# Second layers loaded later, one feature product on GpSimd, and the first rows stored later

## The chip, the cores and the metric

The kernel runs on one core of a Trainium2 chip. The metric is the device time of one execution in microseconds, as the median over several runs. A profile of one execution is used to see what each engine did. In its views the engines are PE (TensorE), PEld (TensorE's weight loads), DVE (VectorE), ACT (ScalarE), POOL (GpSimd) and SP (SyncE); a q behind a name means the queue of that engine, from which it issues DMAs.

## The reference

```python
# attention: batch 4, heads 4, sequence 1088, head size 32, r = 8
def phi(x):                       # 64 features per row: all products of two sketches
    a = einsum('rd,bhsd->bhsr', S1, x);  b = einsum('rd,bhsd->bhsr', S2, x)
    return einsum('bhsi,bhsj->bhsij', a, b).reshape(..., 64)
q_p, k_p = phi(q), phi(k)
kv = einsum('bhsf,bhsd->bhfd', k_p, v);  z = sum(k_p, axis=2)
x = (einsum('bhsf,bhfd->bhsd', q_p, kv) / (einsum('bhsf,bhf->bhs', q_p, z)[..., None] + 1e-6))
x = x.transpose(0, 2, 1, 3).reshape(4352, 128)        # one row per token
# router and experts: 8 experts, 128 -> 1024 -> 128
logits = (x / (|x| + 1e-6)) @ (emb / (|emb| + 1e-6)).T / tau
expert = argmax(logits, 1);  gate = max(softmax(logits))
out[token] = gate[token] * (relu(x[token] @ w1[expert]) @ w2[expert])
```

The inputs are float32, except that S1 and S2 are float64 and are rounded on the chip. Only the expert with the highest score works on a token, so the kernel must sort the tokens by expert while it runs.

## The kernel before, in words

**Attention.** The four batches are taken as two pairs, m = 0 and m = 1. In a pair, tiles of tokens go through in groups of four (GROUPS; the last group has four and one rest tile). For the keys of a group (`keys`) TensorE transposes the rows, multiplies them with the sketch matrix into PSUM (`sketch`), ACT copies one of the two factors to SBUF (`second`, L377), VectorE multiplies the two factors into features of 128x1024 (`features`, L383), and TensorE adds keys times values into an accumulator (L432). For the queries (`queries`) the features are made in the same way (steps `tr`, `ab`, `b`, `prod`), then transposed on TensorE (`tr_qp`, L508), copied to SBUF by ACT (`qpT`, L514) and multiplied with the finished key-value matrix `kz` (`nd`, L522). `x` (L532 to L539) divides by the denominator into the row tile `xg`. The query features of pair 0 are kept in `held`, which is the memory that the second layers of experts 4 to 7 take later.

**Rows and tables.** Each row of `xg` holds 128 values, 8 shifted logits and a scale: `squares` sums squares on ACT (L544) and takes the root on GpSimd (L546); `store` inverts it, for the first eight tiles of a pair on GpSimd (L657, L658) and for the others on VectorE (L654, L655). `write` sends the rows to `rows` in DRAM, by SP (L662), and the rest tile by GpSimd (L666). The router (`best`, `pick`, `place`, `take`, `split`, `mark`) finds the expert of each token on VectorE as a one-hot (`pick`, L613) and its place among the tokens of that expert with a series of small matmuls on TensorE (`place`, L623 to L627, and L753). For pair 0 a table is then worked out (`plan_early`, `table`): `find` and `digit` on VectorE (L718, L722) make `hit` and `col`, `sums` on TensorE (L728) adds them up, and `tokens` on VectorE (L743 to L745) turns the sums into the indices `src_i`, by which full blocks of 128 tokens of one expert can be gathered.

**Experts.** `fetch` gathers a block's rows from `rows` by an indirect DMA on GpSimd (L861). `turn` transposes them (L867), `weights` copies the first layer into the order needed (L874), `up` runs the first layer in 16 passes (L917), `down` the second (L943), and the result goes out by an indirect DMA on GpSimd (L952). There are 36 blocks. The first ten hold tokens of pair 0 alone and start while pair 1 is still in its attention; the others use a second table. Four fetches are put ahead of the first block.

**Loads.** SP issues the loads: keys, queries, values, then all first layers (L180) and the second layers of experts 0 to 3 (L176). The second layers of experts 4 to 7 are eight loads of 256 KB into `held`.

**What sets the order.** Steps are put on a list as functions with a tick and a rank (`put_at(tick)(after, rank, step)`); `emit` runs the list sorted by tick and rank. For the engines that `manual_schedule` names, the instructions stand in the order in which they are emitted; for an engine that it doesn't name, a scheduler places them. In the kernel before, SP is not named. Each engine works off its instructions in order, and an instruction waits until what it reads is ready and what it overwrites has been used.

Of the kernel before, what the change touches and what calls it, by code (L numbers as in the profile page):

```python
# [11 lines left out]
F32 = mybir.dt.float32  # L12
BF16 = mybir.dt.bfloat16
# [6 lines left out]
P = 128  # L20
B, H, S, D = 4, 4, 1088, 32
R = 8
DM = H * D
N = B * S
E, F = 8, 1024
# [38 lines left out]
def kernel(  # L64
# [13 lines left out]
    nc = tc.nc  # L78
# [3 lines left out]
    consts = ctx.enter_context(tc.tile_pool(name="consts", bufs=1))  # L82
    rows_p = ctx.enter_context(tc.tile_pool(name="rows", bufs=4))
    work = ctx.enter_context(tc.tile_pool(name="work", bufs=2))
# [85 lines left out]
    held = w2_sb[:, E // 2:].rearrange("p e f d -> p e (f d)")  # L170

    def load_w2(e):

        for u in range(2):
            f = slice(u * NF // 2, (u + 1) * NF // 2)
            nc.sync.dma_start(w2_sb[:, e, f], w2[e].rearrange("(p f) d -> p f d", p=P)[:, f])  # L176
# [22 lines left out]
    top, rem, w, fits = word("s_top"), word("s_rem"), word("s_w"), word("s_fits")  # L199
# [144 lines left out]
    ND_AT = (range(n_g, 2 * n_g), range(2 * n_g, 3 * n_g))  # L344
# [30 lines left out]
    def second(ab, n, tag):  # L375
        b = tile_of(n, [P, n * H, R], tag)
        nc.scalar.copy(b, ab[:, :, 1])  # L377
        return b

    def features(ab, b, n, tag, t=None):  # L380
        if t is None:
            t = tile_of(n, [P, n, H, R * R], tag)
        nc.vector.tensor_mul(t.rearrange("p j h (i k) -> p (j h) i k", i=R),  # L383
                             ab[:, :, 0].unsqueeze(3).broadcast_to([P, n * H, R, R]),
                             b.unsqueeze(2).broadcast_to([P, n * H, R, R]))
        return t
# [91 lines left out]
    def queries(m, c0, c1, put, put_nd):  # L478
        n = c1 - c0
        w = n * P  # L480
        s = {}
# [12 lines left out]
        def ab():  # L494
            s["ab"] = sketch(ab_bank(put.tick, n, 0), s["qT"], n)

        def b():
            s["b"] = second(s["ab"], n, "qb")

        def prod():  # L500
            t = held[:, c0 // 4].rearrange("p (j h f) -> p j h f", j=4, h=H) if m == 0 and n > 1 else None
            s["qp"] = features(s["ab"], s["b"], n, "qp", t)

        def tr_qp():
            ps = ps_big() if n > 1 else ps_small().rearrange("p (b n) -> p b n", b=2)
# [43 lines left out]
        if m == 0:  # L549
            put(-1, 53, tr)  # L550
            put(0, 50, ab)
            put(0, 50.5, b)
            put(0, 54, prod)
            for i, f in enumerate((tr_qp, qpT)):
                put_nd(*((0, 47.7 + 0.02 * i) if c0 == 0 else (-1, 57)), f)
            put_nd(0, 70, nd)
            put_nd(0, 71.5 if n == 1 else 71, x)
            put_nd(*((1, 55.3 if n == 1 else 53.6) if last else (1, 53.5)), squares)
        else:

            at_rank = ({tr: (7, 53), ab: (7, 70.6), b: (7, 70.7), prod: (7, 71.2), tr_qp: (8, 55.5), qpT: (8, 58),
                        nd: (8, 84), x: (8, 90), squares: (9, 55)},
                       {tr: (8, 53.5), ab: (8, 55.8), b: (8, 58.7), prod: (8, 62.5), tr_qp: (9, 20), qpT: (9, 20),
                        nd: (9, 30), x: (9, 71), squares: (10, 53.5)},
                       {tr: (8, 55.3), ab: (8, 84.6), b: (8, 84.7), prod: (9, 20.2), tr_qp: (9, 30.2), qpT: (9, 30.6),
                        nd: (10, 70), x: (10, 71), squares: (11, 53.5)},
                       {tr: (8, 84.5), ab: (9, 21), b: (9, 30.7), prod: (10, 33), tr_qp: (11, 20), qpT: (11, 20),
                        nd: (11, 70), x: (11, 71), squares: (11, 77)})[min(step, 3)]
            for f, (t, rank) in at_rank.items():
                put_at(t)(0, rank, f)  # L570
        if c1 == s1:

            by = 1 if m == 0 else 2
            bank = (lambda: spare[m, 4 + 4 * by]) if c1 < NC else (lambda: table_bank[m][:, 0])
            best, pick, place, take, split, mark, store, write = router(m, s0, s1, g, bank)

            if m == 0 and c1 < NC:
                at_rank = {best: (0, 80), pick: (0, 81), place: (1, 70.5), take: (1, 71.2), split: (2, 54),
                           mark: (2, 54), store: (2, 54), write: (2, 55)}
            elif m == 0:  # L580
                at_rank = {best: (0, 80), pick: (0, 81), place: (1, 56), take: (1, 56.9), split: (1, 57),
                           store: (1, 57.2), write: (1, 58), mark: (1, 59)}
            elif c1 < NC:
                at_rank = {best: (1, 72), pick: (1, 72), store: (1, 86), write: (1, 90), place: (2, 70.5),
                           take: (2, 71.2), split: (4, 76.5), mark: (5, 76)}
            else:
                at_rank = {best: (1, 31), pick: (1, 31), place: (1, 75.1), take: (1, 76), split: (1, 76),
                           store: (2, 78), write: (2, 90), mark: (6, 32)}
            if c1 == NC:
                put_nd(at_rank[place][0], at_rank[place][1] - 0.1, lambda: table_bank.append(ps_big()))  # L590
            for f, (t, rank) in at_rank.items():
                put_nd(t, rank, f)
# [107 lines left out]
    def table(which, m1, key):  # L700

        n, w = SIZES[which] + which * SHARED, m1 * NCP
        s = {}

        def lie(t):
            return t if which == 0 else t.rearrange("p n w -> p w n")

        def find():  # L710
            if which == 0:
                s["hit"] = consts.tile([P, n, w], BF16, name="hit0")
                s["col"] = consts.tile([P, 2, n, w], BF16, name="col0")
            else:

                s["hit"] = work.tile([P, w, n], BF16, tag="xg", bufs=3, name="hit1").rearrange("p w n -> p n w")
                s["col"] = work.tile([P, w, 2, n], BF16, tag="xg", bufs=3, name="col1").rearrange("p w d n -> p d n w")
            nc.vector.tensor_tensor(out=lie(s["hit"]), in0=lie(key().unsqueeze(2).broadcast_to([P, n, w])),  # L718
                                    in1=lie(bview(place_k, [[0, n], [1, w]])), op=ALU.is_equal)

        def digit(d):
            nc.vector.tensor_mul(lie(s["col"][:, d]), lie(s["hit"]), lie(bview(digits[:, d], [[0, n], [1, w]])))  # L722

        def sums():
            s["ps"] = ps_small()[:, :2 * n]
            tiles = [m * NCP + c for m in range(m1) for c in range(NC)]
            for t in tiles:
                nc.tensor.matmul(s["ps"], row[:, :, t], s["col"].rearrange("p d n w -> p (d n) w")[:, :, t], start=t == tiles[0], stop=t == tiles[-1])  # L728

        def first_rows():  # L730
            s["b"] = consts.tile([HALF, 2, SHARED], BF16, name="halves")
            nc.vector.tensor_copy(s["b"], s["ps"].rearrange("p (d n) -> p d n", d=2)[:HALF, :, LATE:])

        def halves():

            ps = s["ps"].rearrange("p (d n) -> p d n", d=2)
            nc.tensor.matmul(ps[:, :, PAIRS:PAIRS + SHARED], down_half, s["b"], start=False, stop=True, skip_group_check=True)

        def tokens(k0, k1):
            ps = s["ps"].rearrange("p (d n) -> p d n", d=2)  # L740
            rest = column(f"rest{which}_{k0}", w=k1 - k0)
            to = dst_i[which][:, k0:k1]
            nc.vector.tensor_scalar(rest, ps[:, 1, k0:k1], -1.0, float(NOWHERE), op0=ALU.mult, op1=ALU.add)  # L743
            nc.vector.tensor_sub(to, rest, ps[:, 0, k0:k1])
            nc.vector.tensor_scalar_min(src_i[which][:, k0:k1], to, N - 1)  # L745
        return find, lambda: digit(0), lambda: digit(1), sums, tokens, first_rows, halves

    def tokens_by_expert(rounded, out):
# [213 lines left out]
    def put_at(tick):  # L962
        def put(after, rank, f):
            at.setdefault(tick + after, []).append((rank, len(at.get(tick + after, ())), f))
        put.tick = tick
        return put
# [14 lines left out]

    for i in range(n_g):

        put_at(ND_AT[0][-1])(1, 59.6, lambda i=i: load_w2(E // 2 + i))

    count, rest, others = plan_early()
    find, high, low, sums, tokens, *_ = table(0, 1, lambda: early["key"])
# [56 lines left out]

    def emit():
        with tc.manual_schedule(engines={mybir.EngineType.PE, mybir.EngineType.DVE, mybir.EngineType.Activation,
                                         mybir.EngineType.Pool}):
            for i in sorted(at):
                for _, _, f in sorted(at[i], key=lambda x: x[:2]):
                    f()  # L1050
        at.clear()
# [48 lines left out]
```

## Time and profile before

| what | value |
|---|---|
| median of three runs | 212.55 us (211.67 to 212.64) |
| the profiled execution's own time | 212.05 us |
| its span | 210.2 us (1.85 us lie around it) |
| granted TensorE clock | 0.998 of full speed |
| busy: PE, DVE, POOL, ACT | 196.2 (93%), 127.7 (61%), 107.6 (51%), 105.9 (50%) us |
| moved by DMA | 22.68 MB |
| L383, query features of 128x1024 on DVE | 1.21 us each |
| L658 on POOL, 128x8 | 1.67 us |
| loads of w2 and w1 | 32 of 256 KB, median 5.7 us to landing |
| writes of `rows` by SP | 4 of 548 KB, median 5.3 us to landing |
| gathers `xs` from `rows` | 36, median 2.6 us to landing |

All times in views of the trace are microseconds from the start of the span; a line of a timeline gives start, duration, engine, source line, operation, what is written and read, and in brackets how long the engine had been idle before and what ended that. The releaser that is named is the one that came last by the profile; what an instruction really waits for can be another one.

### The profile page before, as it was taken

The page shows a single profiled execution, that of the slowest core. Times are in us where ns is not written, and L with a number is a line of the kernel's source. Part 1 is how long each engine was busy: PE and PEld are TensorE (multiplying, and loading weights), DVE is VectorE, ACT ScalarE, POOL GpSimd, SP SyncE. Part 2 cuts the span into 40 slices and gives each one's busy share as a digit, 9 for nine tenths or more (in the row PEclk, how much of TensorE's full clock was granted, in tenths as well). Part 3 has the DMA queues.
Part 4 walks back from the last instruction along what each step waited for, and adds up shares of the span by engine and source line. Part 5 has one row for each costly group of instructions (what it writes and reads, how often), then busy time and mean ns, then how long its engine had stood idle before and what let it go on. Part 6 is the DMA issues. An engine that isn't in the chain of part 4 may idle for free.

```text
span 210.2 us, 6754 instructions
## 1 busy us (share of the span) xinstructions
PE 196.2 (93%) x2566; PEld 186.5 (89%) x2566; DVE 127.7 (61%) x368; ACT 105.9 (50%) x288; POOL 107.6 (51%) x116
## 2 busy tenths in 40 slices
PE   8969999988879999999999999999999999999991
PEld 7758889966768989998999999999999999999991
DVE  5985476898977786889545453544545356575300
ACT  2544477675559745354243535445353544676430
POOL 4101002163178795741578767676766767752322
PEclk9999999999999999999999999999999999999999
DMA  4979899999611301300111211101111120110000
GB/s 120 327 201 316 220 266 372 346 341 378 235 43 27 125 27 57 134 29 25 25 44 38 56 39 41 40 26 41 34 42 38 38 41 28 41 42 10 7 28 25
DMA packets 18369, 22.68 MB, mean 108 GB/s; under 512 B 5353, under 2 KB 12532, under 8 KB 18336
## 3 DMA queue, kind: packets, MB, share of 16 engines
q1 hardware_dynamic: 15904, 17.33, 25.4%
q0 software_dynamic: 2432, 4.90, 8.9%
q8 instruction: 22, 0.36, 0.8%
q14 instruction: 11, 0.09, 0.1%
HBM read 17.61 MB, written 4.74 MB: 106 GB/s over the span
## 4 chain that ended last, share of the span: by engine, by line
PE 58%; DVE 15%; issue 10%; DMA 4%; SPq 4%; ACT 3%; POOL 3%; POOLq 1%; DVEq 0%; ACTq 0%
PE ps_big L917 22%; PE ps_acc L943 10%; PE ps_ab L943 10%; DMA k_rest<-in_k_dram 3%; PE ps_big L522 2%; PE ps_big L508 2%; SPq L125 2%; PE ps_acc L432 2%; POOL out_dram L952 2%; PE ps_big L922 2%; PE ps_t L867 2%; PE ps_t L728 2%; DVE xg L534 2%; DVE wb L874 2%; SPq L135 1%
## 5 line engine op out<-in xcount | busy, mean ns | idle before, releaser
L952 POOL DMA_INDIRECT out_dram<-y,dst_i x36 | 49.4, 1372 | 37.5 <-ACT y L949 33.4
L917 PE MATMUL ps_big<-xTb,wb 128*128 128x128 f32 x512 | 63.1, 276 | 0.9 <-ACT xTb L870 0.4
L917 PEld LDWEIGHTS ps_big<-xTb,wb 128*128 128x128 f32 x512 | 59.7, 192 | 2.0 <-issue 1.0
L925 ACT ACTIVATE hT<-ps_big 128x1024 f32<-128x1024 f32 x36 | 36.8, 1023 | 48.1 <-PE ps_big L917 46.2
L861 POOL DMA_INDIRECT xs<-rows,src_i x36 | 37.6, 1043 | 19.5 <-issue 12.9
L874 DVE COPY wb<-w_sb 128x1024 f32 x35 | 38.6, 1103 | 11.3 <-issue 9.9
L943 PE MATMUL ps_acc<-w_sb,hT 128*128 x256 | 31.3, 276 | 0.0
L943 PE MATMUL ps_ab<-w_sb,hT 128*128 x256 | 31.2, 275 | 0.0
L943 PEld LDWEIGHTS ps_ab<-w_sb,hT 128*128 128x128 f32 x256 | 29.9, 192 | 0.0
L943 PEld LDWEIGHTS ps_acc<-w_sb,hT 128*128 128x128 f32 x256 | 29.8, 192 | 0.0
L934 DVE TENSOR_SCALAR gate<-gate 128x1 f32<-128x1 f32 x36 | 5.5, 152 | 30.2 <-ACT probs L931 30.2
L546 POOL TENSOR_TENSOR xg<-ssq,half_c 128x4 f32<-128x4 f32 (+1 forms) x10 | 9.8, 984 | 23.8 <-ACT sq L544 23.7
L870 DVE COPY xTb<-ps_t 128x128 f32<-128x128 f32 x30 | 8.7, 290 | 14.5 <-PE ps_t L867 14.4
L949 ACT ACTIVATE y<-ps_ab,gate 128x128 f32<-128x128 f32 x18 | 6.6, 367 | 12.6 <-PE ps_ab L943 11.0
L949 ACT ACTIVATE y<-ps_acc,gate 128x128 f32<-128x128 f32 x18 | 6.6, 367 | 10.4 <-PE ps_acc L943 8.8
L522 PE MATMUL ps_big<-kz,qpT 128*64 128x82 f32 x256 | 10.8, 236 | 0.9 <-issue 0.5
L522 PEld LDWEIGHTS ps_big<-kz,qpT 128*64 128x64 f32 x256 | 9.6, 136 | 2.0 <-issue 1.5
L544 ACT ACTIVATE sq<-xg 128x128 f32<-128x128 f32 x34 | 10.6, 311 | 1.2 <-DVE xg L534 0.4
L867 PE MATMUL ps_t<-ident,xs 128*128 128x128 f32 x36 | 10.2, 283 | 1.0 <-DMA xs<-rows,src_i 1.0
L931 ACT ACTIVATE probs<-xs 128x8 f32<-128x8 f32 x36 | 10.6, 294 | 0.0
L432 PE MATMUL ps_acc<-v,kp 128*64 128x64 f32 x256 | 9.2, 225 | 0.4 <-DVE kp L383 0.4
L432 PEld LDWEIGHTS ps_acc<-v,kp 128*64 128x64 f32 x256 | 8.1, 138 | 1.5 <-issue 0.8
(242 smaller groups left out, 296.4 us busy)
## 6 DMA issues: line engine op xcount, KB each, us to landing
w_sb<-in_moe_w_dram SPq DMA_DIRECT2D x32, 256.0 KB, 5.7
rows<-xg SPq DMA_DIRECT2D x4, 548.0 KB, 5.3
v<-in_v_dram SPq DMA_DIRECT2D x4, 512.0 KB, 6.5
k<-in_k_dram SPq DMA_DIRECT2D x3, 512.0 KB, 5.5
q<-in_q_dram SPq DMA_DIRECT2D x3, 512.0 KB, 5.8
xs<-rows,src_i POOLq DMA_INDIRECT x36, 2.6
out_dram<-y,dst_i POOLq DMA_INDIRECT x36, 2.8
k<-in_k_dram SPq DMA_DIRECT2D x2, 256.0 KB, 3.6
```

Source lines behind the costliest of these rows:

```text
L432: nc.tensor.matmul(acc[m][u * HALF:(u + 1) * HALF, i, p], s["kp"][:, c - c0, h], bass.AP(tensor=vo.tensor, offset=vo.offset, ap=[list(vo.a ...
L522: nc.tensor.matmul(ps[i * HALF:(i + 1) * HALF, j, p * W:(p + 1) * W], s["qpT"][:, p, j * P + i * HALF:j * P + (i + 1) * HALF], kz[m][:, i ...
L544: nc.scalar.activation(sq, xg[g][:, at + j, :DM], ACT.Square, accum_out=ssq[g][:, at + j:at + j + 1])
L861: nc.gpsimd.indirect_dma_start(out=xs[i][:], out_offset=None, in_=rows[:2 * S if t == 0 else N], in_offset=bass.IndirectOffsetOnAxis(ap=sr ...
L867: nc.tensor.transpose(ps[:, :P], xs[i][:, :DM], ident)
L874: copy(to.rearrange("p (f q) -> p f q", f=NF), w1_sb[:, bass.ds(e, 1)].rearrange("p o (q f) -> p (o f) q", f=NF))
L917: nc.tensor.matmul(ps[:, u, j * P:(j + 1) * P], w[:, f * P:(f + 1) * P], x, start=True, stop=True)
L925: nc.scalar.activation(hT[i], ps, ACT.Relu)
L931: nc.scalar.activation(p, xs[i][:, DM:DM + E], ACT.Exp, scale=xs[i][:, ROW - 1:], accum_out=gate[i])
L943: nc.tensor.matmul(ps, h[:, f * P:(f + 1) * P], ws[0][:, f], start=f == 0, stop=f == NF - 1)
L949: nc.scalar.activation(y, ps, ACT.Copy, scale=gate.pop(i)[:, 0:1])
L952: d = nc.gpsimd.indirect_dma_start(out=out[:, :], out_offset=bass.IndirectOffsetOnAxis(ap=dst_i[t][:, j:j + 1], axis=0), in_=y[:], in_offs ...
```

## The change

There are five edits. The eight loads of the last four second layers are put behind the first four gathers in the order of emission (rank 87.2 in the tick of the table, where they had 59.6), and SP is now among the engines whose order is that of emission. `col` of the first table lies in the first quarter of `held`, the place of expert 4's second layer, and no longer in memory of its own. The product of the query features of the first group of pair 1 is made on GpSimd; since it reads both factors from SBUF, ACT copies both (128x256) in place of one (128x128). Their transposes (`tr_qp`) go from rank 55.5 to 56.7, behind the table's matmuls. And `store` and `write` of the first eight tiles of pair 0 are emitted one tick later, behind the roots of the other tiles.

```diff
--- before.py
+++ after.py
@@ -377,10 +377,15 @@
         nc.scalar.copy(b, ab[:, :, 1])
         return b
 
-    def features(ab, b, n, tag, t=None):
+    def both_factors(ab, n):
+        t = work.tile([P, n * H, 2, R], F32, tag="both", bufs=1, name="both")
+        nc.scalar.copy(t, ab)
+        return t
+
+    def features(ab, b, n, tag, t=None, engine=nc.vector):
         if t is None:
             t = tile_of(n, [P, n, H, R * R], tag)
-        nc.vector.tensor_mul(t.rearrange("p j h (i k) -> p (j h) i k", i=R),
+        engine.tensor_mul(t.rearrange("p j h (i k) -> p (j h) i k", i=R),
                              ab[:, :, 0].unsqueeze(3).broadcast_to([P, n * H, R, R]),
                              b.unsqueeze(2).broadcast_to([P, n * H, R, R]))
         return t
@@ -494,12 +499,18 @@
         def ab():
             s["ab"] = sketch(ab_bank(put.tick, n, 0), s["qT"], n)
 
+        by_pool = m == 1 and c0 == 0
+
         def b():
-            s["b"] = second(s["ab"], n, "qb")
+            if by_pool:
+                s["ab"] = both_factors(s["ab"], n)
+                s["b"] = s["ab"][:, :, 1]
+            else:
+                s["b"] = second(s["ab"], n, "qb")
 
         def prod():
             t = held[:, c0 // 4].rearrange("p (j h f) -> p j h f", j=4, h=H) if m == 0 and n > 1 else None
-            s["qp"] = features(s["ab"], s["b"], n, "qp", t)
+            s["qp"] = features(s["ab"], s["b"], n, "qp", t, nc.gpsimd if by_pool else nc.vector)
 
         def tr_qp():
             ps = ps_big() if n > 1 else ps_small().rearrange("p (b n) -> p b n", b=2)
@@ -558,7 +569,7 @@
             put_nd(*((1, 55.3 if n == 1 else 53.6) if last else (1, 53.5)), squares)
         else:
 
-            at_rank = ({tr: (7, 53), ab: (7, 70.6), b: (7, 70.7), prod: (7, 71.2), tr_qp: (8, 55.5), qpT: (8, 58),
+            at_rank = ({tr: (7, 53), ab: (7, 70.6), b: (7, 70.7), prod: (7, 71.2), tr_qp: (8, 56.7), qpT: (8, 58),
                         nd: (8, 84), x: (8, 90), squares: (9, 55)},
                        {tr: (8, 53.5), ab: (8, 55.8), b: (8, 58.7), prod: (8, 62.5), tr_qp: (9, 20), qpT: (9, 20),
                         nd: (9, 30), x: (9, 71), squares: (10, 53.5)},
@@ -576,7 +587,7 @@
 
             if m == 0 and c1 < NC:
                 at_rank = {best: (0, 80), pick: (0, 81), place: (1, 70.5), take: (1, 71.2), split: (2, 54),
-                           mark: (2, 54), store: (2, 54), write: (2, 55)}
+                           mark: (2, 54), store: (3, 55.5), write: (3, 55.6)}
             elif m == 0:
                 at_rank = {best: (0, 80), pick: (0, 81), place: (1, 56), take: (1, 56.9), split: (1, 57),
                            store: (1, 57.2), write: (1, 58), mark: (1, 59)}
@@ -710,7 +721,7 @@
         def find():
             if which == 0:
                 s["hit"] = consts.tile([P, n, w], BF16, name="hit0")
-                s["col"] = consts.tile([P, 2, n, w], BF16, name="col0")
+                s["col"] = held[:, 0, :n * w].bitcast(BF16).rearrange("p (d n w) -> p d n w", d=2, n=n)
             else:
 
                 s["hit"] = work.tile([P, w, n], BF16, tag="xg", bufs=3, name="hit1").rearrange("p w n -> p n w")
@@ -981,7 +992,7 @@
 
     for i in range(n_g):
 
-        put_at(ND_AT[0][-1])(1, 59.6, lambda i=i: load_w2(E // 2 + i))
+        put_at(ND_AT[0][-1])(1, 87.2, lambda i=i: load_w2(E // 2 + i))
 
     count, rest, others = plan_early()
     find, high, low, sums, tokens, *_ = table(0, 1, lambda: early["key"])
@@ -1044,7 +1055,7 @@
 
     def emit():
         with tc.manual_schedule(engines={mybir.EngineType.PE, mybir.EngineType.DVE, mybir.EngineType.Activation,
-                                         mybir.EngineType.Pool}):
+                                         mybir.EngineType.Pool, mybir.EngineType.SP}):
             for i in sorted(at):
                 for _, _, f in sorted(at[i], key=lambda x: x[:2]):
                     f()
```

In the built program this moves the following. On TensorE the eight transposes L508 of that group go from before L447 to after L753, just before L455. On VectorE one L383 is gone. On GpSimd the product stands after the third L546, and L657 and L658 stand after the fifth. On SP both writes of pair 0 stand together, and all eight loads behind them; the first of these waits for the matmuls of `sums`, none waits for a gather. All else keeps its order.

## The prediction

> **What bounds the kernel now.** I read the page's slices first, for where the resources change over; then the busy time by stretch; then the timeline from 36 us to 62 us, where all edits lie; then the DMA issues by window, for how long a transfer lands. For what each instruction waits on I used the order of the two built programs.
>
> The slices show two halves. Their DMA rows:
> ```profile
> DMA  4979899999611301300111211101111120110000
> GB/s 120 327 201 316 220 266 372 346 341 378 235 43 27 125 27 57 134 29 25 25 44 38 56 39 41 40 26 41 34 42 38 38 41 28 41 42 10 7 28 25
> ```
> A slice is 5.25 us. The DMA engines are full until about 56 us and then nearly idle. By stretch (PE, PEld, DVE, ACT, POOL busy, granted clock, DMA share, GB/s):
> ```profile
> 42.00:49.90 7.90, 6.59 (x128) 5.53 (x126) 6.98 (x29) 5.74 (x21) 4.17 (x5) 1.00 1.01 348
> 49.90:57.10 7.20, 6.33 (x118) 5.46 (x113) 6.63 (x23) 3.46 (x5) 1.38 (x2) 1.00 0.88 314
> 57.10:59.80 2.70, 1.10 (x9) 0.86 (x9) 2.15 (x6) 0.54 (x1) 2.05 (x3) 1.00 0.12 29
> 59.80:84.00 24.20, 23.18 (x268) 21.75 (x268) 18.64 (x67) 16.76 (x61) 18.30 (x17) 1.00 0.19 57
> 84.00:186.00 102.00, 101.46 (x1006) 100.46 (x1006) 56.89 (x140) 46.33 (x110) 67.62 (x56) 1.00 0.16 42
> ```
> From 59.8 us on, TensorE is 96% and then 99% busy at the full granted clock. So the end is where the first expert block starts, plus fixed TensorE work: a microsecond won or lost at the first block's transpose (L867, 59.79) is one at the end. Just before it TensorE idles 1.60 of 2.70 us. The timeline shows on what (start, duration, engine, line, and in brackets the idle time before):
> ```profile
> 44.36 1.21 DVE L383 TENSOR_TENSOR qp<-ps_ab,qb 128x1024 f32<-128x1024 f32 x1
> 44.81 0.33 SPq L662 DMA_DIRECT2D rows<-xg  x1
> 45.24 2.68 SPq L176 DMA_DIRECT2D w_sb<-in_moe_w_dram  x4
> 45.62 1.09 PE L508 MATMUL ps_big<-ident,qp 128*128 128x128 f32 x8 [0.56 <-DVE qp L383]
> ...
> 47.90 0.19 PE L623 MATMUL ps_big<-oh,before 128*128 128x72 bf16 x1
> ...
> 50.30 3.25 SPq L176 DMA_DIRECT2D w_sb<-in_moe_w_dram  x4
> ...
> 52.37 1.24 PE L728 MATMUL ps_t<-col,row 128*128 128x20 bf16 x17 [0.46 <-DVE col L722]
> ...
> 57.14 1.06 POOL L861 DMA_INDIRECT xs<-rows,src_i  x1 [5.31 <-DVE lg L539]
> ...
> 59.79 0.33 PE L867 MATMUL ps_t<-ident,xs 128*128 128x128 f32 x1 [0.98 <-DMA xs<-rows,src_i]
> ```
> The transpose waits for the first gather, and the gather was issued at 57.14. DVE L539 is only what ended last before it: the program makes the gather wait for the indices (L745, done 54.22) and for the writes of `rows`. The last of those is a small GpSimd write of L666, issued at 51.28, which landed 5.0 us later, at 56.3. The gather of the late table starts 0.79 us after its indices (100.62 to 101.41), so about 0.8 us lies between release and gather, and 56.3 + 0.8 is 57.1. The writes were late because they shared the queues with eight second-layer loads:
> ```profile
> rows<-xg POOLq DMA_DIRECT2D x1, 34.2 KB, 5.3
> rows<-xg POOLq DMA_DIRECT2D x2, 34.2 KB, 3.4
> ```
> These are L666's landing times at 50.45, among the loads, and at 83.19, without them.
>
> **The change, part by part, on the clock of the trace.**
>
> *Product off VectorE.* L383 at 44.36 goes; the next DVE instruction moves from 45.49 to 44.36, that is 1.13 us earlier, and so does what follows on DVE unless it waits. The one-hot L613 then ends at 46.71 instead of 47.84. TensorE must be free for the table then: it was held by the eight transposes L508 (45.62 to 46.71). These move behind the table, so L447 can go when ACT's copy L440 ends (45.77), the sketch L371 at 46.1, and the table L623 at 46.77 (47.90 less 1.13). VectorE reaches the end of its column products L722 at 51.18 instead of 52.31.
>
> *The moved transposes.* They take the place behind the table, 48.31 less 1.13, that is 47.18 to 48.27. Before, they filled a gap; now TensorE, ACT and TensorE follow on them in series: copy L514 from 48.31 (before 47.41), the small copies L459 0.93 later from 49.24 and done at 49.62, numerators L522 0.10 later at 49.72 (before 49.24), transposes L354 1.29 later at 51.01, ACT's copy of them 51.71 to 52.30, and the table sums L728, which need that PSUM buffer, at 52.35. Before: 52.37. So all 1.13 us that VectorE gains are waited away in front of the sums. Indices (54.20), the second numerators and the third product (56.43) stay where they were, and TensorE reaches the first block's transpose at 57.72 + 1.03 = 58.75, as it did before.
>
> *Product on GpSimd.* It starts at 42.8, when ACT's copy of both factors (0.37 us by the 128x256 copy at 37.16, against 0.27) is done. ACT's next copy waited until 42.96 anyway. No row shows a GpSimd multiply of this size. From below: the memset of 128x328 took 0.38 us and of 128x1 0.10, which makes 1.0 us for 1024 elements written. From above: the affine select of 128x128 took 0.29 us, so 2.3 us for 1024 with one input, and 4.6 if a second input doubles it. I take 3.1, the select's slope above the 0.10 floor, doubled. It then ends at 45.9; its users want it at 47.18, so it is covered up to 4.3 us, and costs 0.3 us at the upper end. Behind it on GpSimd waits the L546 of 45.70, now 45.95 to 46.96; the next L546 waits for ACT until 47.21 anyway. [...]
>
> [...]
>
> *First rows stored later.* L657 and L658 (0.25, 1.67 and gaps, 2.1 in all) move from 42.77 to behind the L546 that ends at 47.76: done at 49.86. The write of the first rows goes from 44.81 to 49.89, the second from 49.88 to 50.32, L666 from 50.45 to 49.95. GpSimd idled from 47.76 to 50.45, so this is free there. SP had no other duty.
>
> *Loads behind.* The eight loads (3.25 us for the last four) leave 45.24 to 53.5. On SP they stand behind both writes and wait for the last sums matmul, about 53.6, because the column products now lie in the place of expert 4's second layer. They do not wait for the gathers. So the writes run alone: the packet records show a lone `rows` write (69.03) moving for 1.65 us, the shared one (49.88) for 3.7, and its end counted 1.1 us after its last packet. Two in a row: 50.31 + 3.3 + 1.1 = 54.7. L666 beside them: 50.8 + 3.4 to 5.0, 54.2 to 55.8. I take 54.7, later than the indices (54.20). The first gather goes at 54.7 + 0.8 = 55.5.
>
> Its landing took 2.6 us on empty queues: 58.1. Now it runs beside the loads: 53.6 to 57, 2.1 MB, which at the 348 GB/s of the stretch above drain until about 60. The nearest row, L666 among the loads, lost 1.6 to 1.9 us: 59.7 to 60.0. But it met over 4 us of queued loads, and the gather meets about 2 (by its packets, 1.35 us after its issue, six are issued at 0.45 us, by the pair at 28.21 in 0.90, and under four drained at 0.75). I take half, 0.9: 59.0, against TensorE's 58.75. The gain is 59.79 - 59.0 = 0.8 us; the ends are 1.04 (TensorE's floor) and -0.2.
>
> [...]
>
> The loads' first user is the first second layer (69.49), some 8 us behind their end. Behind the first transpose the same chain runs earlier: the weight copy on DVE (60.09 to 61.19) does not move, but TensorE wants it only at 64.5, and the fourth product ends 0.5 us earlier, in time. So the gain passes on.
>
> **Sum.** The profiled execution's 212.05 less 0.8 is 211.25. It lay 0.5 below the median of the three runs, so 211.8 for that.
>
> **Rivals.** *The loads eat the gather* (0.22): it loses the whole 1.8 us; between -0.2 and +0.3, 212.6. For it: the L666 row. Against it: the shorter queue.
> *Slower: the GpSimd product is late* (0.15). Place: its transposes at 47.18. It decides from 4.3 us of duration; each further microsecond delays table sums, third product and first block alike. The 1.04 is used up at 5.3 us; at 7 us it costs 1.7, 214.2. For it: two-operand operations on GpSimd are slow in this trace (L658, 1.67 us for eight elements); against it: that is a power, and the add on the same tile took 0.25.
> *More than I add up* (0.10): if the series behind the moved transposes is shorter, so that the sums follow VectorE at 51.2, the gather alone bounds: 58.1, 1.7 us less, 210.9.
> *No effect*: the order on SP and GpSimd does change, so this is part of the first rival.
>
> **Numbers.** Forecast 0.53. About 0.5%, 1.06 us, is what a measurement here can tell from no change. The forecast's ceiling of 1.04 lies at that edge, and the runs before spread by 0.97, so I put 0.22 of its 0.53 beyond it, and nearly all of the 0.10: faster 0.32. The slower rival gives 0.15, the rest is 0.53. The range reaches from most of the faster rival to half of the slower one: 211.0 to 213.3.
>
> **What would show it.** Right: the GpSimd product of 2.3 to 4 us from 42.8, ended before its transposes at about 47.2; table at 46.8; sums still at about 52.4, released by ACT's copy and no longer by DVE; first gather at 55 to 56; first transpose at 58.8 to 59.3. Wrong: a transposes' wait for GpSimd; sums over 0.5 us away from 52.4; a gather released after 56.5; or a first transpose that still waits about a microsecond for its gather.

## The result, and the profile after

The changed kernel takes 217.75 us (median of 4 runs, 217.50 to 218.62); the kernel before took 212.59 (211.67 to 212.87) beside it. The ratio is 1.027 [1.023, 1.031]: slower by 5.2 us, where I had forecast 0.8 us less. Ratios here and below leave out the runs that were over 1.5% above the fastest of their kernel: none of these eight, but five of ten in e4 and at most two of any other changed kernel. The profiled execution took 217.91 us with a span of 216.0, against 212.05 and 210.2.

The page's slices come first: the granted clock, the DMA share and the throughput (a slice is now 5.4 us).
```profile
PEclk9999999999967999999999999999999999999998
DMA  4969899935860031310011111111101111110000
GB/s 125 336 171 352 224 355 370 377 116 184 253 227 16 27 107 33 140 50 15 12 47 45 52 40 38 40 38 33 40 27 44 32 40 40 40 40 10 10 24 26
```
Two things are new. The DMA engines, full until 56 us before, have a hole in the ninth and tenth slices (43 to 54 us) and the missing work in the next two. And the clock falls in the twelfth and thirteenth slices.

By stretch (PE, PEld, DVE, ACT, POOL busy, granted clock, DMA share, GB/s):
```profile
57.60:61.00 3.40, 1.09 (x8) 0.86 (x8) 2.56 (x7) 0.18 (x1) 2.79 (x3) 1.00 0.96 340
61.00:67.80 6.80, 4.21 (x18) 3.77 (x18) 1.92 (x3) 2.94 (x12) 2.36 (x3) 0.50 0.27 93
67.80:92.00 24.20, 23.25 (x273) 22.11 (x272) 18.57 (x76) 14.55 (x50) 17.31 (x18) 1.00 0.21 71
```
TensorE works 1.09 us of the 3.4 ahead of 61, in which the DMA engines are full with loads. Then it has half its clock for 6.8 us, and after that the stretches look as before. The timeline shows the steps of my sum:
```profile
43.16 1.95 POOL L388 TENSOR_TENSOR qp<-both 128x1024 f32<-128x1024 f32 x1
...
47.12 0.19 PE L634 MATMUL ps_big<-oh,before 128*128 128x72 bf16 x1
...
50.27 0.81 SPq L673 DMA_DIRECT2D rows<-xg  x2
...
52.60 1.20 PE L739 MATMUL ps_t<-w_sb,row 128*128 128x20 bf16 x17
...
53.83 3.76 SPq L176 DMA_DIRECT2D w_sb<-in_moe_w_dram  x8
...
57.59 1.06 POOL L872 DMA_INDIRECT xs<-rows,src_i  x1 [6.04 <-DVE lg L550]
...
63.24 0.48 PE L878 MATMUL ps_t<-ident,xs 128*128 128x128 f32 x1 [4.24 <-DMA xs<-rows,src_i]
64.07 3.78 PE L928 MATMUL ps_big<-xTb,wb 128*128 128x128 f32 x16 [0.35 <-ACT xTb L881]
```
The lines have moved by 11 (L867 is L878, L917 is L928; L739 is the table sums, where `col` now has the name of the memory it lies in). TensorE waits 4.24 us for the first gather; the first layer of the first block then takes 3.78 us, where the trace before has 2.04:
```profile
60.49 2.04 PE L917 MATMUL ps_big<-xTb,wb 128*128 128x128 f32 x16 [0.36 <-ACT xTb L870]
```
The gather's landing, from the DMA issues of 57.5 to 57.7:
```profile
xs<-rows,src_i POOLq DMA_INDIRECT x1, 5.6
```
Before, it was 2.6. So the account of the span's 5.8 us: 0.33 at the start (the root L557 begins at 42.00, L546 at 41.67), 0.12 in the gather's issue, 3.00 from its issue to the transpose (5.65 against 2.65), 2.35 from the transpose to the end (152.76 against 150.41).

### The profile page after: what moved, and what is told of

Its sections match the earlier page's. It is cut to its first block, busy times and chain, and to the rows that moved or that the text cites. A ratio compares the mean times of both kernels' runs of the same rounds, so it can differ in the third digit from the quotient of the medians.

```text
span 216.0 us, 6748 instructions
## 1 busy us (share of the span) xinstructions
PE 198.3 (92%) x2566; PEld 188.6 (87%) x2566; DVE 126.9 (59%) x367; ACT 106.1 (49%) x288; POOL 109.7 (51%) x117
## 4 chain that ended last, share of the span: by engine, by line
issue 31%; PE 24%; POOL 16%; DVE 12%; DMA 8%; SPq 4%; ACT 2%; POOLq 2%; DVEq 0%; ACTq 0%
POOL xs L872 9%; PE ps_big L928 8%; POOL out_dram L963 5%; PE ps_big L533 3%; DMA k_rest<-in_k_dram 3%; DMA rows<-xg 3%; DMA xs<-rows,src_i 3%; SPq L125 3%; PE ps_acc L954 3%; PE ps_acc L437 2%; PE ps_big L519 2%; PE ps_ab L954 2%; DVE xg L545 2%; DVE wb L885 2%; DVE kp L388 1%
## 5 line engine op out<-in xcount | busy, mean ns | idle before, releaser
L928 PE MATMUL ps_big<-xTb,wb 128*128 128x128 f32 x512 | 64.8, 281 | 1.2 <-DVE parts L549 0.4
L928 PEld LDWEIGHTS ps_big<-xTb,wb 128*128 128x128 f32 x512 | 61.3, 196 | 2.5 <-issue 1.0
L557 POOL TENSOR_TENSOR xg<-ssq,half_c 128x4 f32<-128x4 f32 (+1 forms) x10 | 9.9, 991 | 28.7 <-ACT sq L555 28.7
L881 DVE COPY xTb<-ps_t 128x128 f32<-128x128 f32 x30 | 8.7, 291 | 15.6 <-PE ps_t L878 15.5
L878 PE MATMUL ps_t<-ident,xs 128*128 128x128 f32 x36 | 10.4, 290 | 4.2 <-DMA xs<-rows,src_i 4.2
L878 PEld LDWEIGHTS ps_t<-ident,xs 128*128 128x128 f32 x36 | 5.3, 147 | 4.9 <-DMA xs<-rows,src_i 4.5
```

The costliest lines, as they stand in the source:

```text
L878: nc.tensor.transpose(ps[:, :P], xs[i][:, :DM], ident)
L928: nc.tensor.matmul(ps[:, u, j * P:(j + 1) * P], w[:, f * P:(f + 1) * P], x, start=True, stop=True)
```

## The experiments

Theory: the gather is held up by the loads that still have bytes to move when it is issued, and the idle time that this makes costs a second time through the clock. Rivals: the rows that are written late do the harm, not the loads; or the product on GpSimd does.

The runs came in three batches, each on another chip (e1 to e4, e5 to e8, e9 to e11), on which the kernel before had medians of 215.72 us (213.58 to 217.70), 212.56 and 212.24; each ratio is against the runs of its own batch. Since the span varies with the start of the run, I split each profiled span at two marks: the issue of the first gather, counted from the first root of the pair (L546 before, L557 in the others), and the first block's transpose.

| kernel | root | root to gather issue | issue to transpose | transpose to end | ratio [95%] |
|---|---|---|---|---|---|
| before | 41.67 | 15.47 | 2.65 | 150.4 | 1 |
| after | 42.00 | 15.59 | 5.65 | 152.8 | 1.027 [1.023, 1.031] |
| e1_gate | 42.09 | 14.93 | 2.70 | 158.7 | 1.024 [1.015, 1.032] |
| e2_warm | 41.63 | 14.85 | 6.18 | 153.5 | 1.012 [1.002, 1.022] |
| e3_loads | 42.13 | 13.22 | 6.08 | 156.1 | 1.020 [1.012, 1.028] |
| e4_early | 41.19 | 16.13 | 2.67 | 152.6 | 0.997 [0.992, 1.001] |
| e5_rest | 42.62 | 15.55 | 2.70 | 152.1 | 1.009 [1.004, 1.013] |
| e6_six_first | 42.28 | 15.57 | 2.70 | 150.5 | 1.004 [0.999, 1.008] |
| e7_four_first | 41.67 | 13.66 | 4.30 | 150.5 | 0.996 [0.992, 0.999] |
| e8_six_pool | 42.35 | 15.89 | 2.75 | 150.4 | 1.004 [1.000, 1.007] |
| e9_gate_four | 41.70 | 13.64 | 3.33 | 150.3 | 0.996 [0.993, 0.999] |
| e10_rest_warm | 42.72 | 15.53 | 2.63 | 150.4 | 1.000 [0.997, 1.004] |
| e11_gate_first | 43.00 | 14.69 | 2.65 | 150.9 | 1.003 [0.999, 1.006] |

**e1_gate.** The changed kernel; SP reads one element of the fourth gather before it issues the loads.
```diff
+    seen = consts.tile([1, 1], F32, name="seen")
+    put_at(ND_AT[0][-1])(1, 87.1, lambda: nc.sync.dma_start(seen[:], xs[AHEAD - 1][:1, :1]))
```


> The changed kernel with one DMA of four bytes added on SP between the four gathers and the eight loads; it copies one element of the fourth gather's rows, so SP issues the loads only when that gather has landed. Theory A (the gathers' packets wait in the DMA engines behind the loads that are issued from 53.8 us on, and the long idle stretch of TensorE that follows halves its clock): first gather issued at 55.5 to 56, landed 2.6 us later, first block's transpose at 58.8 to 59.5, granted clock back at 0.998, 211.5 to 212.5 us. Rival B (the writes of rows, stored late and together, are what delays the gather): the gather is still issued near 57.6 and the first transpose stands at 60.2 or later, 213 us or more. Rival C (the product on GpSimd and the transposes behind the table are the cost): no change, near 217.7.

Its timeline:
```profile
57.02 1.06 POOL L872 DMA_INDIRECT xs<-rows,src_i  x1 [5.37 <-DVE lg L550]
...
59.72 0.33 PE L878 MATMUL ps_t<-ident,xs 128*128 128x128 f32 x1 [0.63 <-DMA xs<-rows,src_i]
60.42 3.38 PE L928 MATMUL ps_big<-xTb,wb 128*128 128x128 f32 x16 [0.37 <-ACT xTb L881]
...
73.91 1.50 PE L954 MATMUL ps_acc<-w_sb,hT 128*128 x8 [2.30 <-DMA w_sb<-in_moe_w_dram]
```
Without the loads the gather is back at 2.70 us and the transpose where it was before; that half of the theory holds. The time did not come back: the gate opened only at 64.5, so that the first second layer waited 2.30 us for its weights, and the clock fell twice. And the gather is still issued at 57.0, with nothing beside the writes of the rows: they land later than I had summed, for a reason of their own.

**e2_warm.** The changed kernel with 14 matmuls of zeros on TensorE ahead of the first transpose.
```diff
+        for _ in range(14 if i == 0 else 0):
+            nc.tensor.matmul(ps[:, :P], zeros, zeros, start=True, stop=True)
         nc.tensor.transpose(ps[:, :P], xs[i][:, :DM], ident)
```


> The changed kernel with 14 extra matmuls of zeros (0.27 us each, 3.8 us) on TensorE just ahead of the first block's transpose, where it idles from 59.0 to 63.2 us. They write a PSUM buffer that the transpose overwrites. Theory A: the gather is as late as before (transpose near 63.2), but TensorE does not idle, so the granted clock stays at 1.0 after it; the first layer of block 0 takes 2.0 us and not 3.8, and the time is 1.7 to 2.4 us shorter than the changed kernel: 215.3 to 216.0. Rival D (the clock has no part in it, the half clock comes from elsewhere, such as the length of the DMA burst): within 0.3 us of 217.7, or slower.

```profile
62.66 0.33 PE L880 MATMUL ps_t<-ident,xs 128*128 128x128 f32 x1 [0.88 <-DMA xs<-rows,src_i]
63.36 2.04 PE L930 MATMUL ps_big<-xTb,wb 128*128 128x128 f32 x16 [0.37 <-ACT xTb L883]
```
The gather takes as long as ever, 6.18 us to the transpose, but the granted clock stays at 1.00 and the first layer runs at full speed. The ratio falls from 1.027 to 1.012. That is over 3 us, more than the clock's 2.35 alone, with intervals of 1% and two different batches; e10 measures this term better.

**e3_loads.** The loads and the order of SP alone: product, transposes, store and write as before.
```diff
-        by_pool = m == 1 and c0 == 0
+        by_pool = False
...
-                           mark: (2, 54), store: (3, 55.5), write: (3, 55.6)}
+                           mark: (2, 54), store: (2, 54), write: (2, 55)}
```


> Only the edit of the loads: eight loads behind the gathers in emission, SP in that order, col in the place of expert 4's second layer; the product is back on VectorE in front of the table, the first rows are stored as early as in the kernel before. Theory A: the gather is issued at about 55 us but meets the loads issued from 53.7 on, lands 3.5 to 5.5 us after its issue, first transpose at 60 to 61, 212.8 to 215 with part of the clock's loss. Rival C (the product and the later stores are the cost): 211.5 to 212.3, since the writes are early and alone and the gather is released earlier.

```profile
54.12 3.93 SPq L176 DMA_DIRECT2D w_sb<-in_moe_w_dram  x8
55.35 1.06 POOL L872 DMA_INDIRECT xs<-rows,src_i  x1 [3.03 <-DVE c_early L785]
...
61.43 0.33 PE L878 MATMUL ps_t<-ident,xs 128*128 128x128 f32 x1 [2.15 <-DMA xs<-rows,src_i]
```
With the rows written early, the gather is issued 2.2 us earlier, released by the indices; and the loads take all of that back: 6.08 us to the transpose. This one edit gives most of the loss. The transpose is a little later than the 60 to 61 us that were expected, and 1.020 is well above the expected times: behind the transpose the clock falls here too, from 63.6 to 67.1, and there are further waits that stay open (below).

**e4_early.** The changed kernel with the loads of experts 5 to 7 ahead of the rows' writes; only those of expert 4, whose place `col` holds, stay behind the sums.
```diff
-        put_at(ND_AT[0][-1])(1, 87.2, lambda i=i: load_w2(E // 2 + i))
+        put_at(ND_AT[0][-1])(*((1, 87.2) if i == 0 else (0, 30)), lambda i=i: load_w2(E // 2 + i))
```


> The changed kernel with the six loads of experts 5 to 7 put ahead of both writes of rows on SP, where the DMA engines were idle from 46 to 51 us; only the two loads of expert 4, whose place holds col, stay behind the sums. Theory A: six loads drain by 49 to 50 us, the writes run alone, the two loads at 53.8 drain by 55.5, before the first gather's packets, so it lands in 2.6 us: first transpose at 58.8 to 59.5, clock 0.998, 211.3 to 212.3 us, faster than the kernel before. Rival B: gather issued near 57, 212.5 to 213.5. Rival C: near 217.7.

In the trace the loss is gone: 2.67 us from issue to transpose and no fall of the clock; the ratio can't be told from 1. It is not gone in every execution. In five of the ten runs the mean granted clock was 0.995 to 0.999 and the time 212.9 to 215.7 us; in the other five it was 0.989 to 0.991 and the time 216.9 to 217.7. The gather is issued late (57.32, 16.1 us behind the root): the two writes go out 8.3 us behind the root as in e1, but have six loads ahead of them on the queue and two behind.

**e5_rest.** The other half: product on GpSimd, late transposes, late stores; loads and SP as before.
```diff
-        put_at(ND_AT[0][-1])(1, 87.2, lambda i=i: load_w2(E // 2 + i))
+        put_at(ND_AT[0][-1])(1, 59.6, lambda i=i: load_w2(E // 2 + i))
...
-                s["col"] = held[:, 0, :n * w].bitcast(BF16).rearrange("p (d n w) -> p d n w", d=2, n=n)
+                s["col"] = consts.tile([P, 2, n, w], BF16, name="col0")
...
-                                         mybir.EngineType.Pool, mybir.EngineType.SP}):
+                                         mybir.EngineType.Pool}):
```


> The other half of the change alone: product of query features on GpSimd, its transposes later, first rows stored later; loads, their rank, the place of col and the free order of SP as in the kernel before. The order of SP becomes: three second-layer loads, the two late writes of the rows (about 50.3), five loads right behind them. Theory Q (the gather is held up by loads that are under way): the writes go first in their queue and land at about 56.2 as in the run with the gate; the five loads (1.3 MB at 350 GB/s) move from about 54.5 to 58.5; the gather is issued at 57, its packets move at 59 or later, it lands at about 60.5 to 61.5; ratio 1.005 to 1.015, and up to 1.025 if the clock drops. Theory W (what hurts in the full change is that the rows are written late, not the loads): gather issued at 57, landing 2.6 us, first transpose at 59.8 as before, ratio 1.000. Theory E (only the loads edit is at fault, this half is free): the gather issued at 55.5, ratio 0.995 to 1.0.

The gather is issued 15.55 us behind the root, as before, and lands as before; five loads behind the writes had 0.60 MB left when it was issued. Yet 152.1 us follow instead of 150.4. The stretches of e5 show why:
```profile
58.80:62.20 3.40, 1.78 (x14) 1.36 (x13) 2.41 (x5) 0.97 (x2) 2.72 (x3) 1.00 0.47 147
62.20:65.60 3.40, 3.40 (x24) 3.07 (x24) 1.85 (x3) 2.81 (x12) 2.00 (x3) 0.51 0.20 46
```
Busy for 1.78 of 3.4 us, TensorE gets half its clock for the next 3.4, which costs half of the 3.40 us in it, 1.7. The ratio lies in theory Q's range, but Q had the gather held up by the five loads, which it was not; that the range was met is luck. The ten runs of e5 part by the clock: seven with a mean clock of 0.984 to 0.991 took 214.0 to 216.0 us, three with 0.997 took 212.65 to 213.0, and the kernel before 212.56.

**e10_rest_warm.** The same with five matmuls of zeros ahead of the first transpose (the edit of e2_warm with 5).
```diff
+        for _ in range(5 if i == 0 else 0):
+            nc.tensor.matmul(ps[:, :P], zeros, zeros, start=True, stop=True)
```


> As the run with the product and the late stores alone, and five matmuls of zeros (about 1.2 us) ahead of the first block's transpose, which fill the wait for the gather. Theory C (that run lost its 1.7 us behind the first transpose to the lower clock alone): no drop of the granted clock, the first layer of the first block takes 2.0 instead of 3.2 us, from the first transpose to the end 150.5 us as in the kernel before instead of 152.1; ratio 0.998 to 1.003. Rival (something else in that half slows the blocks): still 151.5 or more from the transpose to the end, ratio 1.006 to 1.010.

```profile
58.80:62.20 3.40, 2.96 (x24) 2.60 (x24) 2.48 (x5) 0.96 (x3) 2.79 (x3) 1.00 0.32 105
62.20:65.60 3.40, 3.17 (x49) 2.84 (x48) 2.18 (x5) 3.27 (x15) 2.00 (x3) 1.00 0.18 46
```
The same stretches, at the same distance from the root within 0.1 us, keep the full clock; 150.4 us follow, and the ratio goes from 1.009 to 1.000. All ten runs had a mean clock of 0.994 or more. So that half of the change costs nothing that shows here but the clock, and the clock's part is shown by itself.

**e6_six_first, e7_four_first.** e3 with six loads, or four, right behind the first write of the rows, and the other two, or four, behind the sums (the first added line is e6, the second e7).
```diff
-        put_at(ND_AT[0][-1])(1, 87.2, lambda i=i: load_w2(E // 2 + i))
+        put_at(ND_AT[0][-1])(*((1, 87.2) if i == 0 else (0, 56)), lambda i=i: load_w2(E // 2 + i))
+        put_at(ND_AT[0][-1])(*((1, 87.2) if i < 2 else (0, 56)), lambda i=i: load_w2(E // 2 + i))
```


> Loads and SP order alone (product and stores as in the kernel before), but the six loads of experts 5 to 7 stand right behind the first write of the rows, and only the two of expert 4 behind the sums. Theory Q: six loads issued 45.3 to 49.2, drained at about 52; the second write (50.3) moves right behind them and lands by 55; the two late loads (53 to 53.8) are through by 56; the gather is released by the indices (55.4) or half a microsecond later, and lands in 2.6 to 3.2 us; first transpose at TensorE's own floor, about 58.8, no drop of the clock; ratio 0.993 to 0.997. Theory W (late rows are what hurts): the same. Rival: any load behind the gather's release costs the whole 2 us: first transpose at 60.5 to 61, ratio 1.003 to 1.008. Rival: the second write among six loads still lands at 56.3 as before, gather at 57.1, ratio 1.000.

> As the run with six loads first, but four (experts 6 and 7) behind the first write and four (experts 4 and 5) behind the sums. Theory Q, a dose: four loads issued 53.5 to 55.2 drain at about 57.5 to 58; the gather is issued at 55.4 and its landing lies between that with two late loads (about 2.8) and that with eight (about 6), at 4 to 4.5: first transpose at 59.5 to 60; ratio 0.997 to 1.003, without a drop of the clock. Rival (the number of late loads does not matter, only that some are ahead): landing 6, first transpose at 61.4 as with all eight, ratio 1.01 to 1.02. Theory W: landing 2.6, ratio 0.995.

e6 went as its last rival: the second write stands behind six loads, the gather is issued as late as before, and nothing is won. In e7 the writes are through early. Its timeline and the gather's landing:
```profile
55.33 1.06 POOL L872 DMA_INDIRECT xs<-rows,src_i  x1 [3.47 <-DVE rc L544]
...
59.63 0.33 PE L878 MATMUL ps_t<-ident,xs 128*128 128x128 f32 x1 [0.82 <-DMA xs<-rows,src_i]
```
```profile
xs<-rows,src_i POOLq DMA_INDIRECT x1, 4.3
```
Issued as early as in e3, with four loads under way instead of eight, it lands in 4.3 us: a dose, as the theory had it. The packet records of seven traces put numbers on it. They count what second-layer loads had still to move when the gather was issued (in e3 and e2 some of these were issued after it), and the time until the gather's own first packet moved:

| kernel | loads left, MB | issue to its first packet, us | issue to transpose, us |
|---|---|---|---|
| e1_gate | 0 | 1.76 | 2.70 |
| e10_rest_warm | 0.42 | 1.76 | 2.63 |
| e5_rest | 0.60 | 1.76 | 2.70 |
| e7_four_first | 0.95 | 2.32 | 4.30 |
| after | 1.49 | 3.59 | 5.65 |
| e2_warm | 1.81 | 4.07 | 6.18 |
| e3_loads | 2.07 | 3.77 | 6.08 |

At some 350 GB/s (the stretch ahead of 61 us has 340), what is gone within the gather's own 1.76 us is 0.6 MB, and up to that the loads cost nothing that shows: 2.63 and 2.70 us to the transpose in e10 and e5, 2.70 in e1. What lies above it would drain in 1.0, 2.5, 3.5 and 4.2 us (e7, after, e2, e3); the transpose came 1.6, 3.0, 3.5 and 3.4 us later than with no loads left. So the cost is about the draining time, but not for the last of the loads: in e3 the gather's packets were through by 60.9, with 0.46 MB still to move.

**e8_six_pool.** e6 with the product on GpSimd and its transposes behind the table, the stores early.
```diff
-        by_pool = False
+        by_pool = m == 1 and c0 == 0
...
-            at_rank = ({tr: (7, 53), ab: (7, 70.6), b: (7, 70.7), prod: (7, 71.2), tr_qp: (8, 55.5), qpT: (8, 58),
+            at_rank = ({tr: (7, 53), ab: (7, 70.6), b: (7, 70.7), prod: (7, 71.2), tr_qp: (8, 56.7), qpT: (8, 58),
```


> As the run with six loads first, and the product of query features on GpSimd with its transposes behind the table, the first rows still stored early. My prediction's own step says that the 1.13 us that VectorE gains are waited away in front of the table sums: sums at 52.4 as without it, first transpose the same within 0.3 us, ratio equal to that of the run with six loads first within 0.2%. Rival: the series behind the moved transposes is shorter and the sums come up to 1.1 us earlier: first transpose at 57.7 to 58.5, ratio 0.5% lower. Rival: the product behind the stores on GpSimd (44.9 to 46.9) delays the roots by 1.2 us and with them the second write: gather up to 1 us later, ratio 0.3 to 0.5% higher.

Nothing won: ratio 1.004, as e6. But this is no clean test of the prediction's step, which has the sums at the same time with and without the product. The GpSimd product now stands behind the stores and ends at 47.4; the first transpose is 0.4 us later after the root than in e6, and the sums 0.7 (53.81 against 53.03, roots at 42.35 and 42.28).

**e9_gate_four.** e7, with the four late loads behind the landing of the second gather.
```diff
+    seen = consts.tile([1, 1], F32, name="seen")
+    put_at(ND_AT[0][-1])(1, 87.1, lambda: nc.sync.dma_start(seen[:], xs[1][:1, :1]))
```


> As the run with four loads first and four behind the sums, but the four late loads stand behind the landing of the second gather: SP reads one element of it before it issues them. Theory Q: nothing lies beside the first gather, so that it is issued at 55.4 (released by the indices), lands in 2.6 us at 58.0, and the first transpose is at TensorE's own floor, 58.8, 0.8 to 0.9 us earlier than with the four loads ungated; the loads go at 59.3 to 61.7 and are there by 65.5, ahead of the first second layer; ratio 0.990 to 0.994, 0.004 below the ungated run. Rival: the loads only collide with the third and fourth gathers, and the wait comes back there (transposes of 67 and 73): ratio as the ungated one or higher, 0.996 to 1.002. Rival: the first second layer waits for the loads as it did behind the gate on the fourth gather: 1.0 us or more at 69, ratio over 1.0.

```profile
55.34 1.06 POOL L872 DMA_INDIRECT xs<-rows,src_i  x1 [3.47 <-DVE rc L544]
...
58.67 0.27 PE L878 MATMUL ps_t<-ident,xs 128*128 128x128 f32 x1
...
59.30 2.05 PE L928 MATMUL ps_big<-xTb,wb 128*128 128x128 f32 x16 [0.35 <-ACT xTb L881]
```
The transpose no longer waits: it follows its predecessor on TensorE, and the first block starts 1.15 us sooner after the root than before. The span is 209.0 against 210.2; the ratio is 0.996 [0.993, 0.999], so this version beats both kernels, by little. The trace shows 0.96 us against e7; the two ratios do not show it, their intervals are wider than that.

**e11_gate_first.** e1 with the gate on the first gather.
```diff
-    put_at(ND_AT[0][-1])(1, 87.1, lambda: nc.sync.dma_start(seen[:], xs[AHEAD - 1][:1, :1]))
+    put_at(ND_AT[0][-1])(1, 87.1, lambda: nc.sync.dma_start(seen[:], xs[0][:1, :1]))
```


> The changed kernel with the gate of the earlier run, but on the first gather instead of the fourth: the eight loads wait for the first gather alone. Theory Q: gather issued at 57.0 (the rows written late), landed 2.6 us later, first transpose at 59.7; loads issued 60.4 to 64, there by 68, so that the first second layer does not wait: ratio 1.000 to 1.003 with the clock kept, 1.008 to 1.010 if the clock drops for one step of 3.4 us as it did behind the gate on the fourth gather. Rival: the gate itself is what cost that run its time: ratio still 1.02.

All five edits stand, and only the eight loads start at 61.1 instead of 53.8; the ratio is 1.003 [0.999, 1.006]. The transpose waits 0.35 us for its gather, the first second layer 0.25 us for the loads, and the clock holds. So neither the gate as such nor the late rows made e1 slow. Of the 8.3 us by which its trace is longer than the trace before behind the transpose, 3.4 are two stretches at half clock and 2.3 the wait for the weights, which the gate on the fourth gather made; most of the rest are the further waits that stay open.

## Why the prediction was wrong, step by step

Times are put on the clock of the trace before (0.33 us less). The first transpose was predicted at 59.0 and came at 62.91. Of these 3.9 us, 1.8 are the gather's later issue (57.26, not 55.5) and 2.1 its longer landing (5.65 us to the transpose, not 3.5). The clock added 2.35 us behind it.

*VectorE, table and sums: right.* Table at 46.79 (46.77 predicted), sums at 52.27 (52.35), the third product's transposes done at 58.66 (58.75). The 1.13 us that VectorE gained were waited away in front of the sums: its column products were done at 51.22 (51.18 predicted).

*Product on GpSimd: right, with a wrong size.* It took 1.95 us where I took 3.1; both lie under the cover of 4.3.

*First rows later: the landing was mis-sized.* Stores were done at 49.91 (49.86). But the step "Two in a row: 50.31 + 3.3 + 1.1 = 54.7" counted the two writes from their issue. In e1, with nothing beside them, the first packet moved 0.8 us after the first issue (at 51.19 on e1's own clock), 95% had begun to move by 54.3, the last ended at 55.6, and the gather was issued at 57.0, which puts the release at about 56.2: 1.5 us more than the step had. In the changed kernel the first loads' packets lay beside the last ones, and the gather went at 57.26, where 55.5 was predicted. The early write that was moved away is worth 2 us where the second one does not stand behind the loads, as it did before the change: e3, e7 and e9 issue the gather at 55.3.

*The gather beside the loads: the step that failed.* "I take half, 0.9: 59.0". It lost 3.0. The eight loads drained at 62.2, where "drain until about 60" was the estimate, since they began to move at 54.5 beside the last of the rows and moved 0.38 MB in their first 2.1 us. The backlog at the time of the gather's packets was near what I had taken: 1.49 MB at its issue, less 1.76 us at 350 GB/s, is 0.87 MB or 2.5 us. (The reading that the gather's packets move 1.35 us after its issue was off: in the trace before they begin 1.75 us after it, at 58.89.) Wrong was to halve the loss of the L666 row because the queue was half as long. That row was a write of 34 KB that shared the queues; a loss of 1.9 us there was no upper end for a gather. The table above shows a loss near the draining time of what is ahead: 3.0 us in the changed kernel, where 2.5 us were left to drain.

*The clock: no term held it.* I had read the 1.60 us of idle time ahead of the first block as time lost once. With a wait of 4.24 us it costs again: the clock was at half for 6.8 us, in which TensorE was busy 4.21, so this is 2.1 of the 2.35 us. In the other traces it was low for 3.4 us in e5 and e3, and for 3.4 us at two places in e1; the 6.8 us of the changed kernel are twice that in a row. In these four traces the changes of the clock lie a whole number of steps of 3.41 us apart (the two falls in e1, at 60.87 and 74.52 us, four steps), but the steps lie differently to the root: one begins 14.7 us behind it in e3, 15.4 in e1, 15.6 in the changed kernel and 16.2 in e5.

*Rivals.* "The loads eat the gather" was the mechanism, with a price of 1.8 us and no slower end than 212.6; it should have carried the draining time of all eight loads, and the clock behind it. The slower rival that I had priced (a late GpSimd product) did not happen.

What stays open: in the traces of e2, e3 and e4, and in e1 besides its wait for the weights, TensorE waits a further 1.8 to 2.9 us between the first transpose and 92 us (1.1 of it for the one-hot at 76 in e4), which no trace of the later batches shows. The kernel before was 3 us slower in that batch too, but its trace there is not at hand. How much idle time brings the fall stays open too. Counted in these steps, the idle time of the kernel before ahead of its first layer is spread over two of them (busy 2.25 and 2.56 of 3.41 us), that of e1 lies in one (1.86), and the clock fell in e1 alone. But near that value it goes either way: the steps ahead of the other falls were busy for 1.09 to 1.14 us (after, e3, and the second in e1) and for 1.79 (e5), while 1.74 in e6 and 1.82 in e4 brought none.
```profile
57.07:60.48 3.41, 1.74 (x28) 1.34 (x22) 2.82 (x7) 1.22 (x1) 2.02 (x2) 1.00 0.25 76
60.48:63.89 3.41, 2.97 (x34) 2.63 (x36) 2.59 (x4) 2.88 (x13) 2.41 (x2) 1.00 0.21 46
```
These are e6's two stretches. Seven of its twelve runs had a mean clock of 0.981 to 0.992 and took 213.2 to 216.6 us, the other five 211.9 to 213.0: whether the clock falls differs between executions of one kernel.

## What to carry to other kernels

Before bulk loads are moved behind a step, work out how many bytes they will still have to move when the next small gather or write on the path is issued, and charge that gather their whole draining time beyond its own start-up (1.76 us here), not a share; here the loss was 0.8 to 1.6 times that (e2, e3, e7 and the changed kernel). A gate on the first landing (e11, ratio 1.003 [0.999, 1.006]), or moving part of the loads to where the queues have room (e7, 0.996 [0.992, 0.999]), cost nothing that could be measured here, since their user came late enough. And where TensorE's wait grows by microseconds, add a second price that may come: half of the work behind the wait at half clock, which was 1.7 us in e5 (3.4 us at half clock) and 2.1 us in the changed kernel (6.8 us). Five matmuls of zeros in the gap took that price away in e10.

## What the runs showed of the hardware

- A gather on GpSimd's queue was held up by loads on SP's queue that were issued before it or just after: its first packet moved 1.76 us after issue with 0 to 0.60 MB of them left (e1, e10, e5), 2.32 us with 0.95 MB (e7), 3.6 to 4.1 us with 1.5 to 2.1 MB (the changed kernel, e2, e3).
- Idle time of 1.6 us in a stretch of 3.4 (e5) was followed by half a clock over the next 3.4 us, at a cost of 1.7 us; with five matmuls of zeros (1.28 us, e10) the clock stayed at 1.00. As much idle time in e6 (1.7 us) was not followed by a fall.
- The feature product of 128x1024 took 1.95 us on GpSimd (the changed kernel, 43.16) against 1.21 on VectorE (the kernel before, 44.36).
- Two writes of 548 KB issued together on empty queues took 5.4 us to landing (median of e1), issued apart 3.6 (median of e3). In e1 the last packet ended 1.3 us after 95% had begun to move.
